# Written order for attention's last pair, a five-step decode of the first expert block, and a halved last output tile

## The chip, the cores and the metric

The kernel runs on one core of one Trainium2 chip. The metric is the device time of one execution in microseconds; lower is better. Engines are named as in the profile: PE (matrix products), DVE (vector), ACT (scalar), POOL (GpSimd) and SP, which here only issues transfers.

## What is computed

Clustered attention (2 batches, 8 heads, 768 positions, head dimension 64), then two dense expert layers on the 1536 tokens:

```python
mask = q_assign[:, :, :, None] == k_assign[:, :, None, :]     # nearest of 16 centroids
scores = np.where(mask, scale * np.matmul(q, k.transpose(0, 1, 3, 2)), -1e9)
attn = softmax(scores);  x = (attn @ v) as [1536, 512]
x = leaky_relu(x @ w_in1, 0.01) @ w_out1                       # 512 -> 2048 -> 512
out = relu(x @ w_in2) ** 2 @ w_out2
```

All inputs are float32. Every product is made from a rounded high part and a rest (names ending in h and l), so each expert product is three matmuls and each attention-times-values product is two.

## The kernel before

**Attention.** Two heads form a pair; there are NP = 8 pairs. A head's 768 queries go in three units of 256, so a pair has UPP = 6 units and there are NU = 48. A step u of the loop at line 712 runs one line of the table PLAN, in which an entry `Name:lag` calls the operation for unit u - lag. The operations of a unit are, with their engine: S0, S1 (PE, L389: scores of 128 queries, tile S, two buffers); R0, R1 (DVE, L412: row maximum nm); X0, X1 (ACT, L422: exponential e); RE (ACT, L433) and RC (DVE, L436: reciprocal r of the row sums); N0, N1 (POOL, L439: normalise e); Ta, Tb, Tc (PE, L452: four transpositions each into tile T, three buffers); Ha, Hb, Hc (ACT, L463: high part eh); La, Lb, Lc (DVE, L469: rest el); Va, Vb, Vc (PE, L487: four matmuls each into tile A, one buffer); FC (ACT, L500) and FA (DVE, L509), which add A's two halves into xt. With the lags, step u computes scores of unit u + 1, transpositions of u - 2 and products A of u - 3; FA is that of u - 4, and the A of u - 3 starts only when that FA has freed the one buffer. The first three units of a pair belong to its first head and their FA uses partitions 0 to 63, the last three belong to the second head and use 64 to 127. In the first seven pairs, steps also prepare the next pair (dots, cluster ranks L318 to L339, splits). When a pair is done, xsplit (L205, L517 on POOL) splits its xt into xh and xl.

**Who sets the order.** Inside `manual_schedule` each engine's queue stands as the calls are written. Outside, a scheduler sets it by its own estimates. SP is in written order throughout. For the other four engines the first manual block ends at line 719, at step 42, that is ahead of the last pair; a second starts at expert step (0, 2). Between them the scheduler decides.

**Expert blocks.** A weight block (128 x 1024 float64) arrives as raw integer words wraw (one buffer, L147) and is decoded by seven pieces (decode_pieces, L138): load (SP), mag (ACT, L156), shift (DVE, L160), low (DVE, L166), sign (DVE, L173), high (ACT, L133, makes wh) and the rest (POOL, L134, makes wl). For block 0, one piece each follows steps 42 to 46 and two follow step 47 (lines 737 to 741). The load of the next block waits for a small POOL copy of the reciprocals of unit 45 into wraw (L205). The first layer's products h (L770) then fill PE between the last units of attention, as the scheduler places them.

**Output.** g2 (L829) makes four output tiles o of 128 x 512 for a token block, each from two blocks f with three matmuls per f (L847). After the second f, flush (L857) adds o to acc on DVE (L874 for the last step of the second layer) and SP sends 256 KB (L876). Twelve such transfers form the result.

Of the kernel before, what the change touches and what calls it, by code (L numbers as in the profile page):

```python
# [53 lines left out]
def attention_moe_moe_kernel(  # L54
# [9 lines left out]
    nc = tc.nc  # L64
# [7 lines left out]
    NF = w1.shape[0]  # L72
    NU = NP * 2 * (KC // 2)
    UPH = KC // 2
    HALF = S // 2
    N = 512
    NBLK = NT // N
    PLAIN = (3, 2)
    EARLY = 1
# [58 lines left out]
    def decode_pieces(ci):  # L138

        m, f, j = blocks[ci]  # L140
        st = {}

        def load():
            st["raw"] = stg[0].tile([128, 2 * DM, 2], I32, tag="wraw", name="wraw")
            if ci == EARLY:
                pool_copy(out=st["raw"][:, 0].bitcast(F32), in_=r_t[NU - 3])
            nc.sync.dma_start(  # L147
                out=st["raw"].rearrange("p a b -> p (a b)"), in_=(w1, w2)[m][f + j].bitcast(I32)
            )

        def mag():
            pool = stg[0] if j == 0 or ci < 2 else stg[1]
            t = pool.tile([128, 2 * DM], I32, tag="wt", name="wt")
            st["t"] = t
            words[ci] = t.bitcast(F32)
            nc.scalar.mul(out=t.bitcast(F32), in_=st["raw"][:, :, 1].bitcast(F32), mul=W_SHIFT)  # L156

        def shift():
            t = st["t"]
            nc.vector.tensor_scalar(  # L160
                out=t, in0=t, scalar1=3, scalar2=None, op0=ALU.logical_shift_left
            )

        def low():
            t = st["t"]
            nc.vector.scalar_tensor_tensor(  # L166
                out=t, in0=st["raw"][:, :, 0], scalar=29, in1=t,
                op0=ALU.logical_shift_right, op1=ALU.bitwise_or,
            )

        def sign():
            t = st["t"]
            nc.vector.scalar_tensor_tensor(  # L173
                out=t, in0=st["raw"][:, :, 1], scalar=-0x80000000, in1=t,
                op0=ALU.bitwise_and, op1=ALU.bitwise_or,
            )

        def high():
            st["rest"] = split_block(ci, st["t"].bitcast(F32))

        return [load, mag, shift, low, sign, high, lambda: st["rest"]()]
# [22 lines left out]
    def pool_copy(out, in_):  # L204
        nc.gpsimd.tensor_scalar(  # L205
            out=out, in0=in_, scalar1=1.0, scalar2=1.0, op0=ALU.mult, op1=ALU.mult
        )
# [313 lines left out]
    UPP = 2 * UPH  # L521
# [186 lines left out]
        "pl11": lambda p: place(p, 1, 1),  # L708
    }

    early = [f for i in range(EARLY) for f in decode_pieces(i)]
    for u in range(-1, NU + 5):
        if u == NU - UPP:
            pst.close()
            stg.append(ctx.enter_context(tc.tile_pool(name="stg", bufs=1, side="right", reuse_waits="tile")))
            wpx = ctx.enter_context(tc.tile_pool(name="wpx", bufs=SIDE, side="right", reuse_waits="tile"))
            ring.append((wpx, SIDE))
        if u == NU - 6:
            manual.close()
        p = u // UPP  # L720
        for op in PLAN[FIRST[u] if p == 0 else u % UPP].split():
            if ":" in op:
                name, lag = op.split(":")
                i = u - int(lag)
                if 0 <= i < NU and (name, i) != ("RC", 0):
                    unit_ops[name](i)
                    for f in hooks.get((name, i), ()):
                        f()
            else:
                name, ahead = op.split("@")  # L730
                q = p + 1 + int(ahead)
                if name in ("xhi", "xlo"):
                    if 0 <= q - 2 < NP - 1:
                        xsplit(q - 2, name == "xlo")
                elif 0 < q < NP and not (q == 1 and name in PRE):
                    prep_ops[name](q)
        w = u - (NU - UPP)
        if w >= 0:
            k = len(early)
            for f in early[k * w // UPP : k * (w + 1) // UPP]:  # L740
                f()
    xsplit(NP - 1, 0)
    xsplit(NP - 1, 1)
    ast.close()
# [10 lines left out]
    acc = accp.tile([128, NBLK, 4, N], F32, name="acc")  # L755
# [3 lines left out]
    def tmp(tag="q", bufs=6):  # L759
        return gp.tile([128, N], F32, tag=tag, name=tag, bufs=bufs)  # L760

    def bank(i):
        return ps_h.tile([128, N], F32, tag=f"h{i}", name="h")
# [63 lines left out]
    outs = {}  # L827

    def g2(m, b, f):  # L829
        first, last = f % 2 == 0, f % 2 == 1  # L830
        wh, wl = weights[m, f // 2 * 2, f % 2]
        gh, gl = parts.pop((m, b, f))
        for o in range(4):
            if first:
                outs[o] = (ps_l if o == 3 else ps_o).tile([128, N], F32, tag=f"o{o}", name="o")
            if m == 0:
                ws = slice(DM + o * 128, DM + (o + 1) * 128)
                mm = ((wh[:, ws], gh), (wh[:, ws], gl), (wl[:, ws], gh))
            else:
                ts = slice(o * 128, (o + 1) * 128)  # L840
                mm = (
                    (gh[:, ts], wh[:, DM:]),
                    (gh[:, ts], wl[:, DM:]),
                    (gl[:, ts], wh[:, DM:]),
                )
            for i, (l, r) in enumerate(mm):
                nc.tensor.matmul(  # L847
                    out=outs[o],
                    lhsT=l,
                    rhs=r,  # L850
                    start=(first and i == 0),
                    stop=(last and i == 2),
                )
            if last:
                flush(m, b, f // 2, o, outs[o])

    def flush(m, b, g, o, ps):  # L857
        a = acc[:, b, o]
        if g == 0:
            nc.scalar.copy(out=a, in_=ps)  # L860
            return
        if g < NF // 2 - 1:
            nc.vector.tensor_tensor(out=a, in0=ps, in1=a, op=ALU.add)  # L863
            return
        if m == 0:
            c = slice(b * N, (b + 1) * N)
            nc.vector.tensor_tensor(out=a, in0=ps, in1=a, op=ALU.add)
            nc.scalar.copy(out=xh[:, o, c], in_=a)
            nc.gpsimd.tensor_tensor(
                out=xl[:, o, c], in0=a, in1=xh[:, o, c].bitcast(F32), op=ALU.subtract  # L870
            )
        else:
            ob = tmp()
            nc.vector.tensor_tensor(out=ob, in0=ps, in1=a, op=ALU.add)  # L874
            r = b * N + o * 128
            nc.sync.dma_start(out=out[r : r + 128, :], in_=ob)  # L876

    def quad(m, f):
        f0, f1, s = ((m, f, j) for j in range(3))
# [232 lines left out]
```

## Time and profile before

| what | value |
| --- | --- |
| three runs | 762.56 us median, 762.07 to 762.88 |
| the profiled execution | 762.55 us, of which the span of its instructions is 760.8 us |
| PE busy | 746.1 us, 98% of the span |
| DVE busy | 569.7 us, 75% |
| ACT busy | 440.4 us, 58% |
| POOL busy | 383.4 us, 50% |
| granted TensorE clock | 1.000 of full speed |

Busy time counts a matmul until its result is written, and consecutive matmuls overlap, so a busy PE may still issue below its pace. The pace is read from the start of one instruction to that of the next. Of the profile's views, the chain of waits tells what released each instruction on the way to the end, the timeline gives start and duration of single instructions (a row may merge equal ones that follow each other), and the table by stretches gives each engine's busy time between two moments.

### The profile page before, as it was taken

The page shows a single profiled execution, that of the slowest core. Times are in us where ns is not written, and L with a number is a line of the kernel's source. Part 1 is how long each engine was busy: PE and PEld are TensorE (multiplying, and loading weights), DVE is VectorE, ACT ScalarE, POOL GpSimd, SP SyncE. Part 2 cuts the span into 40 slices and gives each one's busy share as a digit, 9 for nine tenths or more (in the row PEclk, how much of TensorE's full clock was granted, in tenths as well). Part 3 has the DMA queues.
Part 4 walks back from the last instruction along what each step waited for, and adds up shares of the span by engine and source line. Part 5 has one row for each costly group of instructions (what it writes and reads, how often), then busy time and mean ns, then how long its engine had stood idle before and what let it go on. Part 6 is the DMA issues. An engine that isn't in the chain of part 4 may idle for free.

```text
span 760.8 us, 11079 instructions
## 1 busy us (share of the span) xinstructions
PE 746.1 (98%) x4060; PEld 650.0 (85%) x4060; DVE 569.7 (75%) x861; ACT 440.4 (58%) x812; POOL 383.4 (50%) x344
## 2 busy tenths in 40 slices
PE   8999999999999999999999999999999999999998
PEld 8899999999989888888888888887878888888886
DVE  5999999999999545876666576656678787686755
ACT  6988988988998564344444343546544345443430
POOL 2889889889855326561442314356461441423400
PEclk9999999999999999999999999999999999999999
DMA  7494563572601212111121112203111211122004
GB/s 230 96 219 110 123 167 107 123 170 69 154 23 61 107 56 111 55 56 56 59 108 56 55 56 84 83 1 111 56 56 61 94 68 55 56 77 90 1 1 165
DMA packets 16902, 66.35 MB, mean 87 GB/s; under 512 B 3152, under 2 KB 4048, under 8 KB 11856
## 3 DMA queue, kind: packets, MB, share of 16 engines
q1 hardware_dynamic: 16848, 65.65, 29.1%
q8 instruction: 32, 0.52, 0.3%
q14 instruction: 22, 0.18, 0.1%
HBM read 44.60 MB, written 3.15 MB: 63 GB/s over the span
## 4 chain that ended last, share of the span: by engine, by line
PE 78%; DVE 13%; ACT 5%; issue 1%; DMA 1%; POOL 1%; DVEq 0%; SPq 0%; ACTq 0%; POOLq 0%
PE o L847 32%; PE h L770 29%; PE A L487 6%; PE S L389 5%; PE T L452 5%; DVE el L469 4%; DVE nm L412 3%; ACT e L422 2%; DMA wraw<-w 1%; PE warm L242 1%; DVE xt L509 1%; DVE ds L319 1%; ACT acc L860 1%; DVE m L318 1%; DVE h L806 1%
## 5 line engine op out<-in xcount | busy, mean ns | idle before, releaser
L134 POOL TENSOR_TENSOR wl<-wt,wh 128x1024 fp32r<-128x1024 f32 x32 | 77.0, 2407 | 132.8 <-ACT wh L133 132.8
L818 DVE TENSOR_TENSOR gl<-h,gh 128x512 fp32r<-128x512 f32 x96 | 65.8, 690 | 70.8 <-ACT h L813 50.2
L770 PE MATMUL h<-xl,wh 128*128 128x512 f32 x296 | 115.4, 390 | 0.0
L770 PE MATMUL h<-xh,wl 128*128 128x512 f32 x296 | 115.0, 389 | 0.0
L770 PE MATMUL h<-xh,wh 128*128 128x512 f32 x296 | 114.8, 390 | 0.0
L863 DVE TENSOR_TENSOR acc<-o,acc 128x512 f32<-128x512 f32 x144 | 92.6, 685 | 12.1 <-PE o L847 12.1
L469 DVE TENSOR_TENSOR el<-T,eh 128x512 fp32r<-128x512 f32 x144 | 94.4, 683 | 4.3 <-ACT eh L463 3.2
L439 POOL TENSOR_SCALAR e<-e,r 128x768 f32<-128x768 f32 x96 | 87.7, 925 | 19.4 <-DVE r L436 13.2
L412 DVE TENSOR_REDUCE nm<-S 128x1 f32<-128x768 f32 x96 | 90.9, 948 | 4.2 <-PE S L297 2.4
L422 ACT ACTIVATE e<-S,nm 128x768 f32<-128x768 f32 x96 | 87.3, 909 | 11.0 <-DVE nm L412 6.8
L389 PE MATMUL S<-hb 128*128 128x384 f32 (+1 forms) x384 | 90.2, 349 | 1.9 <-ACT e L422 1.2
L463 ACT CAST eh<-T 128x512 fp32r<-128x512 f32 x144 | 79.8, 589 | 13.4 <-PE T L452 13.1
L487 PE MATMUL A<-eh,vv 128*128 128x256 f32 x288 | 79.6, 306 | 2.0 <-DVE xt L509 2.0
L452 PE MATMUL T<-ident,e 128*128 128x128 f32 x576 | 79.6, 273 | 1.0 <-DVE el L469 1.0
L847 PE MATMUL o<-wh,gh 128*128 128x512 f32 x192 | 75.0, 391 | 2.8 <-DVE acc L863 1.7
L847 PE MATMUL o<-gl,wh 128*128 128x512 f32 x192 | 74.8, 390 | 0.0
L847 PE MATMUL o<-wh,gl 128*128 128x512 f32 x192 | 74.7, 389 | 0.0
L847 PE MATMUL o<-gh,wl 128*128 128x512 f32 x192 | 74.7, 389 | 0.0
L847 PE MATMUL o<-wl,gh 128*128 128x512 f32 x192 | 74.7, 389 | 0.0
L847 PE MATMUL o<-gh,wh 128*128 128x512 f32 x192 | 73.6, 389 | 0.0
L487 PE MATMUL A<-el,vv 128*128 128x256 f32 x288 | 72.5, 282 | 0.4 <-DVE el L469 0.4
L452 PEld LDWEIGHTS T<-ident,e 128*128 128x128 f32 x576 | 69.0, 144 | 4.0 <-POOL e L439 1.3
(130 smaller groups left out, 1537.1 us busy)
## 6 DMA issues: line engine op xcount, KB each, us to landing
wraw<-w SPq DMA_DIRECT2D x32, 1024.0 KB, 4.7
hb<-spl SPq DMA_DIRECT2D x14, 576.0 KB, 4.7
hb<-spl SPq DMA_DIRECT2D x42, 192.0 KB, 5.1
rqk<-qk SPq DMA_DIRECT2D x16, 384.0 KB, 3.8
rv<-v SPq DMA_DIRECT2D x8, 384.0 KB, 3.6
out<-q SPq DMA_DIRECT2D x12, 256.0 KB, 2.0
twice<-qk SPq DMA_DIRECT2D x8, 192.0 KB, 6.3
hb<-st SPq DMA_DIRECT2D x56, 24.0 KB, 2.0
```

The lines of the kernel that those rows point to most:

```text
L134: return lambda: nc.gpsimd.tensor_tensor(out=wl, in0=t, in1=wh.bitcast(F32), op=ALU.subtract)
L389: nc.tensor.matmul(out=s[:, c, 0:HALF], lhsT=hb[0:k, a, i * 128 : (i + 1) * 128], rhs=hb[0:k, b, c * HALF : (c + 1) * HALF], start=(a == 0 ...
L412: nc.vector.tensor_reduce(out=n, in_=s_t[t][:, :, 0:HALF], axis=AX.XY, op=ALU.max, negate=True)
L422: nc.scalar.activation(out=e.rearrange("p (a b) -> p a b", a=2), in_=s_t.pop(t)[:, :, 0:HALF], func=AF.Exp, bias=n_t.pop(t), scale=1.0, ac ...
L439: nc.gpsimd.tensor_scalar(out=e_t[t], in0=e_t[t], scalar1=r_t[t // 2][:, t % 2 : t % 2 + 1], scalar2=1.0, op0=ALU.mult, op1=ALU.mult,)
L452: nc.tensor.transpose(T[:, o : o + 128], e_t[2 * u + b][:, kc * 128 : (kc + 1) * 128], ident)
L463: nc.scalar.copy(out=eh[:, 2 * g : 2 * g + 2, :].rearrange("p a b -> p (a b)"), in_=T_t[u, g])
L469: nc.vector.tensor_tensor(out=el[:, 2 * g : 2 * g + 2, :].rearrange("p a b -> p (a b)"), in0=T_t.pop((u, g)), in1=eh[:, 2 * g : 2 * g + 2, ...
L487: nc.tensor.matmul(out=A, lhsT=w, rhs=m[:, kc, :], start=(kc == 0 and i == 0), stop=(kc == KC - 1 and i == 1),)
L770: nc.tensor.matmul(out=out, lhsT=l, rhs=r, start=(first and i == 0), stop=(i == n - 1), skip_group_check=not first,)
L847: nc.tensor.matmul(out=outs[o], lhsT=l, rhs=r, start=(first and i == 0), stop=(last and i == 2),)
L863: nc.vector.tensor_tensor(out=a, in0=ps, in1=a, op=ALU.add)
```

## The change

Three edits. The first manual block is left at step 47 and not at 42, so that the queues of PE, DVE, ACT and POOL keep the written order for steps 42 to 46. The pieces that decode block 0 are called in the middle of a step, behind Lc: load and mag in step 42, shift in 43, low in 44, sign in 45, high and rest in 46, nothing in 47. And of the last output tile (second layer, last token block, last f pair, o = 3) the 512 columns are made as two halves of 256 in two PSUM banks, each with its own matmuls, addition and transfer of 128 KB.

```diff
--- before.py
+++ after.py
@@ -708,14 +708,15 @@
         "pl11": lambda p: place(p, 1, 1),
     }
 
-    early = [f for i in range(EARLY) for f in decode_pieces(i)]
+    early = decode_pieces(0)
+    early_at = (early[0:2], early[2:3], early[3:4], early[4:5], early[5:7], ())
     for u in range(-1, NU + 5):
         if u == NU - UPP:
             pst.close()
             stg.append(ctx.enter_context(tc.tile_pool(name="stg", bufs=1, side="right", reuse_waits="tile")))
             wpx = ctx.enter_context(tc.tile_pool(name="wpx", bufs=SIDE, side="right", reuse_waits="tile"))
             ring.append((wpx, SIDE))
-        if u == NU - 6:
+        if u == NU - 1:
             manual.close()
         p = u // UPP
         for op in PLAN[FIRST[u] if p == 0 else u % UPP].split():
@@ -726,6 +727,9 @@
                     unit_ops[name](i)
                     for f in hooks.get((name, i), ()):
                         f()
+                if name == "Lc" and NU - UPP <= u < NU:
+                    for f in early_at[u - (NU - UPP)]:
+                        f()
             else:
                 name, ahead = op.split("@")
                 q = p + 1 + int(ahead)
@@ -734,11 +738,6 @@
                         xsplit(q - 2, name == "xlo")
                 elif 0 < q < NP and not (q == 1 and name in PRE):
                     prep_ops[name](q)
-        w = u - (NU - UPP)
-        if w >= 0:
-            k = len(early)
-            for f in early[k * w // UPP : k * (w + 1) // UPP]:
-                f()
     xsplit(NP - 1, 0)
     xsplit(NP - 1, 1)
     ast.close()
@@ -831,6 +830,7 @@
         wh, wl = weights[m, f // 2 * 2, f % 2]
         gh, gl = parts.pop((m, b, f))
         for o in range(4):
+            split = (m, b, f // 2, o) == (1, NBLK - 1, NF // 2 - 1, 3)
             if first:
                 outs[o] = (ps_l if o == 3 else ps_o).tile([128, N], F32, tag=f"o{o}", name="o")
             if m == 0:
@@ -843,19 +843,25 @@
                     (gh[:, ts], wl[:, DM:]),
                     (gl[:, ts], wh[:, DM:]),
                 )
-            for i, (l, r) in enumerate(mm):
-                nc.tensor.matmul(
-                    out=outs[o],
-                    lhsT=l,
-                    rhs=r,
-                    start=(first and i == 0),
-                    stop=(last and i == 2),
-                )
-            if last:
-                flush(m, b, f // 2, o, outs[o])
-
-    def flush(m, b, g, o, ps):
-        a = acc[:, b, o]
+            todo = [(outs[o], slice(0, N))]
+            if split:
+                if first:
+                    outs[4] = bank(0)
+                todo = [(outs[3 + j][:, 0 : N // 2], slice(j * N // 2, (j + 1) * N // 2)) for j in range(2)]
+            for ps, c in todo:
+                for i, (l, r) in enumerate(mm):
+                    nc.tensor.matmul(
+                        out=ps,
+                        lhsT=l,
+                        rhs=r[:, c],
+                        start=(first and i == 0),
+                        stop=(last and i == 2),
+                    )
+                if last:
+                    flush(m, b, f // 2, o, ps, c)
+
+    def flush(m, b, g, o, ps, part):
+        a = acc[:, b, o, part]
         if g == 0:
             nc.scalar.copy(out=a, in_=ps)
             return
@@ -870,10 +876,10 @@
                 out=xl[:, o, c], in0=a, in1=xh[:, o, c].bitcast(F32), op=ALU.subtract
             )
         else:
-            ob = tmp()
+            ob = tmp()[:, part]
             nc.vector.tensor_tensor(out=ob, in0=ps, in1=a, op=ALU.add)
             r = b * N + o * 128
-            nc.sync.dma_start(out=out[r : r + 128, :], in_=ob)
+            nc.sync.dma_start(out=out[r : r + 128, part], in_=ob)
 
     def quad(m, f):
         f0, f1, s = ((m, f, j) for j in range(3))
```

**DVE, steps 42 to 44 of the last pair.** nm is a row maximum, el a rest of a transposed tile, xt is FA, r a reciprocal; wt is the block being decoded. Before:

```order
L160 TENSOR_SCALAR wt_3367<-wt_3367 128x1024
L469 TENSOR_TENSOR el_3260<-T_3270,eh_3259 128x512
L166 SCALAR_TENSOR_TENSOR wt_3367<-wraw_3304,wt_3367 128x1024
L509 TENSOR_TENSOR xt_3098<-A_3253,xt_3098 64x256
L412 TENSOR_REDUCE nm_3325<-S_3293 128x1
L469 TENSOR_TENSOR el_3260<-T_3299,eh_3259 128x512
L436 RECIPROCAL r_3249<-r_3249 128x2
L173 SCALAR_TENSOR_TENSOR wt_3367<-wraw_3304,wt_3367 128x1024
L412 TENSOR_REDUCE nm_3352<-S_3328 128x1
```

The change, from `shift` in step 43 to behind `low` in step 44:

```order
L160 TENSOR_SCALAR wt_3266<-wt_3266 128x1024
L469 TENSOR_TENSOR el_3324<-T_3307,eh_3323 128x512
L412 TENSOR_REDUCE nm_3354<-S_3330 128x1
L469 TENSOR_TENSOR el_3324<-T_3335,eh_3323 128x512
L509 TENSOR_TENSOR xt_3098<-A_3317,xt_3098 64x256
L436 RECIPROCAL r_3313<-r_3313 128x2
L412 TENSOR_REDUCE nm_3388<-S_3358 128x1
L469 TENSOR_TENSOR el_3324<-T_3364,eh_3323 128x512
L166 SCALAR_TENSOR_TENSOR wt_3266<-wraw_3264,wt_3266 128x1024
L469 TENSOR_TENSOR el_3386<-T_3369,eh_3385 128x512
```

The three operations on wt stood within eight rows; now each is alone in its step, behind one el and ahead of another.

**POOL, end of the last pair.** Rows on e normalise two tiles of a unit (e_3436 is the first of unit 45 in both); xh and xl split the seventh pair's xt; wl is the rest of block 0. Before:

```order
L134 TENSOR_TENSOR wl_3608<-wt_3367,wh_3607 128x1024
L439 TENSOR_SCALAR e_3311<-e_3311,r_3312 128x768
L439 TENSOR_SCALAR e_3338<-e_3338,r_3312 128x768
L205 TENSOR_SCALAR xh_66<-xt_3098 128x768
L439 TENSOR_SCALAR e_3374<-e_3374,r_3375 128x768
L439 TENSOR_SCALAR e_3401<-e_3401,r_3375 128x768
L517 TENSOR_TENSOR xl_67<-xt_3098,xh_66 128x768
L439 TENSOR_SCALAR e_3436<-e_3436,r_3437 128x768
L439 TENSOR_SCALAR e_3463<-e_3463,r_3437 128x768
L205 TENSOR_SCALAR wraw_3764<-r_3437 128x2
```

The change:

```order
L439 TENSOR_SCALAR e_3374<-e_3374,r_3375 128x768
L205 TENSOR_SCALAR xh_66<-xt_3098 128x768
L439 TENSOR_SCALAR e_3402<-e_3402,r_3375 128x768
L517 TENSOR_TENSOR xl_67<-xt_3098,xh_66 128x768
L205 TENSOR_SCALAR wraw_3764<-r_3437 128x2
L134 TENSOR_TENSOR wl_3519<-wt_3266,wh_3518 128x1024
L439 TENSOR_SCALAR e_3436<-e_3436,r_3437 128x768
L439 TENSOR_SCALAR e_3464<-e_3464,r_3437 128x768
```

The row on wl stood ahead of unit 43's normalisation; it now stands ahead of unit 45's, behind the split of the seventh pair and the copy into wraw.

**PE, behind the last scores.** S_3546 and S_3550 are unit 47's second score tile; T tiles that read e_3436 are unit 45's transpositions; A_3572 is unit 44's product. Before:

```order
L452 MATMUL T_3558<-ident_70,e_3436 128x128
L452 MATMUL T_3558<-ident_70,e_3463 128x128
L452 MATMUL T_3558<-ident_70,e_3436 128x128
L452 MATMUL T_3558<-ident_70,e_3463 128x128
L389 MATMUL S_3546<-hb_3002 128x384 x4
L452 MATMUL T_3580<-ident_70,e_3436 128x128
L452 MATMUL T_3580<-ident_70,e_3463 128x128
```

The change:

```order
L452 MATMUL T_3556<-ident_70,e_3402 128x128
L452 MATMUL T_3562<-ident_70,e_3436 128x128
L452 MATMUL T_3584<-ident_70,e_3436 128x128
L487 MATMUL A_3572<-eh_3512,vv_3079 128x256
L487 MATMUL A_3572<-el_3513,vv_3079 128x256
```

Unit 45's first transpositions stood ahead of the last scores, where now they stand behind them; they are still ahead of unit 44's product.

## Rows read from the trace of the kernel before

**Rows 1.** The page, part 4: the chain that ended last, by engine.

```profile
PE 78%; DVE 13%; ACT 5%; issue 1%; DMA 1%; POOL 1%; DVEq 0%; SPq 0%; ACTq 0%; POOLq 0%
```

**Rows 2.** Busy time by stretch: us, PE, PEld, DVE, ACT, POOL, clock, DMA, GB/s.

```profile
205.16:209.33 4.17, 4.17 (x34) 4.10 (x33) 4.17 (x8) 4.02 (x11) 4.12 (x4) 1.00 0.57 175
...
262.00:510.00 248.00, 248.00 (x1095) 205.07 (x1094) 158.90 (x206) 114.87 (x180) 98.35 (x67) 1.00 0.18 64
```

**Rows 3.** The chain in order of time (start, us, what): pieces on PE.

```profile
206.49 0.95 PE A L487 x8
...
207.44 0.71 PE S L389 x4
...
208.15 0.88 PE T L452 x8
...
286.78 2.72 PE o L847 x12
```

**Rows 4.** Busy time of PE from unit 38 to the second output block.

```profile
208.78:267.34 58.56, 57.23 (x372) 1.00 0.19 69
```

**Rows 5.** Timeline of PE (start, us, engine, line, op, tiles, idle before): its two idle spells.

```profile
220.25 0.38 PE L487 MATMUL A<-el,vv 128*128 128x256 f32 x1 [0.35 <-DVE el L469]
...
223.00 1.23 PE L452 MATMUL T<-ident,e 128*128 128x128 f32 x8 [0.98 <-DVE el L469]
```

**Rows 6.** Timeline of DVE: R1 of steps 38, 39, 40 and 42, a pair of rests.

```profile
196.20 0.96 DVE L412 TENSOR_REDUCE nm<-S 128x1 f32<-128x768 f32 x1
...
200.51 0.96 DVE L412 TENSOR_REDUCE nm<-S 128x1 f32<-128x768 f32 x1
...
204.47 0.93 DVE L412 TENSOR_REDUCE nm<-S 128x1 f32<-128x768 f32 x1
...
212.44 0.94 DVE L412 TENSOR_REDUCE nm<-S 128x1 f32<-128x768 f32 x1
...
213.54 0.69 DVE L469 TENSOR_TENSOR el<-T,eh 128x512 fp32r<-128x512 f32 x1 [0.16 <-ACT eh L463]
```

**Rows 7.** The chain in order of time: pieces on DVE, and a product behind one.

```profile
195.05 0.46 DVE m L330
...
195.55 0.44 DVE xt L509
...
196.03 0.74 PE A L487 x4
...
215.61 0.68 DVE wt L160
...
216.90 1.13 DVE wt L166
...
220.27 1.12 DVE wt L173
```

**Rows 8.** Timeline of ACT, steps 42 and 43: mag, a high part, an exponential.

```profile
213.88 1.16 ACT L156 ACTIVATE wt<-wraw 128x1024 f32<-128x1024 f32 x1
...
214.91 0.60 ACT L463 CAST eh<-T 128x512 fp32r<-128x512 f32 x1
...
216.82 0.90 ACT L422 ACTIVATE e<-S,nm 128x768 f32<-128x768 f32 x1
```

**Rows 9.** Timeline of POOL in the last pair, and one DVE row beside it.

```profile
212.37 1.79 POOL L439 TENSOR_SCALAR e<-e,r 128x768 f32<-128x768 f32 x2 [1.89 <-PE S L389]
...
220.44 2.61 POOL L439 TENSOR_SCALAR e<-e,r 128x768 f32<-128x768 f32 x2 [6.28 <-DVE r L436]
...
223.02 2.38 POOL L134 TENSOR_TENSOR wl<-wt,wh 128x1024 fp32r<-128x1024 f32 x1
...
241.09 1.17 DVE L160 TENSOR_SCALAR wt<-wt 128x1024 int32<-128x1024 int32 x1 [0.45 <-ACT wt L156]
```

**Rows 10.** Timeline of the end, and transfers: issuer, count, KB each, us to landing.

```profile
755.69 2.37 SPq L876 DMA_DIRECT2D out<-q  x4
...
out<-q SPq DMA_DIRECT2D x12, 256.0 KB, 2.0
```

## The prediction

> **What bounds the kernel now.** I read the page's chain first: 78% of it is PE and 13% DVE [rows 1], so the order of work on PE decides, and DVE only where PE waits for it. The table by stretches then says where PE has room. From 262 to 510 us it is busy for all of 248.00 us [rows 2], at full clock; behind the place of the change nothing can be caught up, so a delay (or gain) at attention's end moves the end of the kernel by the same amount. What has to be weighed is the stretch from the last pair to the first expert products.
>
> There PE's own pace comes from starts on the chain: eight products A take 0.95 us (0.119 each), four scores 0.71 (0.178), eight transpositions 0.88 (0.110), twelve expert products 2.72 (0.227) [rows 3]. A unit of 12 A, 12 T and 8 S is 4.17 us of PE, and the stretch of that length in the written order shows PE busy throughout [rows 2]. From the first A of unit 38 to the first o of the second output block 58.56 us go by [rows 4]. In them lie 120 A, 105 T, 48 S and 96 h or o: 14.25 + 11.55 + 8.52 + 21.76 = 56.08 us. So the scheduler's order loses **2.5 us** there; 1.3 of it is visible as two waits of PE for DVE's rests el [rows 5], the rest is smaller than a view shows. This is all that a better order could win here.
>
> The rival resource is DVE. From one step's first row maximum to the next it takes 200.51 to 204.47, 3.96 us, and 196.20 to 200.51, 4.31, where FA belongs to a pair's second head [rows 6]. Against 4.17 DVE has only 0.2 us to spare in the former and is over in the latter. Before, the scheduler placed the decoding among shifted work; in the written order it comes on top of a full step.
>
> **The inserts on DVE.** Steps 43, 44 and 45 carry FA of units 39 to 41 (second head), 46 that of unit 42 (first head). The three inserted operations take some 0.60 (the next starts 0.60 after the shift's start; its row says 0.68), 1.13 and 1.12 us [rows 7]. In step 42 nothing is added on DVE, but mag stands on ACT between Ha and X1. It starts at 213.88 and holds ACT until 214.91, 1.03 us [rows 8]. Behind it X1 (0.90) and Hb (0.60) end at 214.91 + 1.50 = 216.41, and DVE, free for that el at 215.61 [rows 7], waits 0.80. A further 0.16 is the wait for ACT of the first el of this step [rows 6], which I keep. From R1 of step 42 at 212.44 [rows 6], which the change does not touch, R1 comes at
> - step 43: 212.44 + 4.31 + 0.16 + 0.80 = 217.71
> - step 44: + 4.31 + 0.60 = 222.62
> - step 45: + 4.31 + 1.12 = 228.05
> - step 46: + 3.96 + 1.12 = 233.13
>
> FA stands just ahead of R1, and A has one buffer. That PE feels a late FA at once is seen in an ordinary pair: a mask operation of 0.46 us on DVE, FA at 195.55, and A at 196.03 directly behind it [rows 7]. So unit 43's first A comes at about 233.1. At PE's pace it would come five units after unit 38's, at 208.78 + 5 x 4.17 = 229.63 [rows 2, 4]. **Lost: 3.5 us.** X1 behind mag also delays a score tile by some 0.25; that lies within these 3.5.
>
> **Step 46.** `high` is a pass over 128 x 1024 on ACT like mag, so about 1.03 us [rows 8]; it stands ahead of X1, which frees the S buffer for unit 47's second scores. By the pace these would start at 233.1 + 0.48 + 0.71 + 0.44 + 0.95 = 235.7; they come about 0.2 later. Then `rest` runs on POOL, from about 235.2 for 2.38 us [rows 9], to 237.6; behind it in POOL's queue is unit 45's normalisation, the first of a pair that takes 1.79 [rows 9], so about 0.9, to 238.5. In PE's order unit 45's transpositions come directly behind the last scores and ahead of unit 44's products. The scores end near 236.0 + 0.71 + 0.44 = 237.1, so PE waits **1.4 us**, and nothing stands in its queue that could go first. Together with the 0.2: 1.6. Then h products cover what DVE still has to do. The other moved work (xl of the seventh pair, the copy into wraw, the second block's load) runs in front of that point or under 21 h products (21 x 0.227 = 4.8 us); I cost it at nothing, and price the case in which that cover is too short as a rival.
>
> **DVE beside POOL.** No row shows an inserted operation at its new place. By the steps above each starts some 0.3 us before POOL ends a normalisation pair. A shift at 241.09 beside one took 1.17 instead of 0.68; a normalisation pair beside `sign` took 2.61 instead of 1.79 [rows 7, 9]. One of two therefore waits. The bounds are 0 (POOL gives way each time) and 3 x 0.3 = 0.9; I take **0.6**, since the shift's row is the nearest and shows DVE giving way, by more than 0.3. The Trainium skill, "SBUF — State Buffer", section "SBUF: two separate sides", says that a DVE operation with two SBUF inputs (or in a two-port mode) and a GpSimd operation share a pair of ports by an exclusive lock: the one that starts first keeps it for its whole instruction, and the other stands still. By that rule each of the three inserts waits out its 0.3, the term is 0.9 and the time would be 766.0; the trace agrees so far that 2.61 is 1.79 + 0.82.
>
> **The halved tile.** Three products of 512 columns, 3 x 0.227 = 0.68 us, become six of 256, each like an A product: 6 x 0.119 = 0.71, so +0.03 for a pass and +0.07 for its two passes [rows 3]. The last addition begins as late as before but is half as long. SP hands on the last transfers about 0.6 us apart (four in 2.37 [rows 10]), mostly at the pace of the additions, and one transfer more costs it up to that. A transfer of 256 KB lands 2.0 us after its issue [rows 10]; no row shows one of 128 KB at the end. Bounds: -0.4 (half an addition and a little of the landing saved) to +0.4 (a further issue, nothing saved). I take **-0.1**.
>
> **Sum.** 3.5 + 1.6 + 0.6 - 2.5 - 0.1 = +3.1 us. The profiled execution took 762.55 us, as good as the median of 762.56, so the forecast is **765.7 us**. A change of 0.2%, 1.5 us, is about what this measurement can tell from none: 761.0 to 764.1 counts as the same.
>
> **Rivals.**
> - *Faster: the buffers absorb the inserts.* S has two buffers and T three. If PE can run ahead on transpositions and scores while FA is late, DVE's debt of each insert is paid in parts, only some 0.5 us of the 2.5 stay lost, and the time is 762.55 - 2.0 = **760.5**. It decides whether FA's lateness reaches A, that is whether an insert plus a DVE step exceeds 4.17; even the smallest, 3.96 + 0.60, does, and the A at 196.03 waited at once [rows 7]. For it speaks that the written order ran PE without a gap in every step before [rows 2]. 8%.
> - *No change.* The three waits that no row shows at their new place do not occur: mag's 0.8, the port's 0.6, the 1.4 for `rest`. Then +3.1 - 2.8 = +0.3, **762.9**. For it speaks that each depends on a few tenths of timing on another engine; against it, that all three would have to go. 18%.
> - *Worse: the second block is late.* Its load waits for the copy of unit 45's reciprocals, which now stands behind the split of the seventh pair on POOL, and its decoding must then pass DVE and POOL. If the 21 h products end first, PE waits about a `rest` of 2.38 less what is left of them, some 2 us: **767.7**. Against it: the copy stands ahead of `rest`, and 4.8 us is more than one pass of any engine. 6%.
>
> **How the numbers follow.** My case has 68%, with a range of its own of 764.2 to 767.0: the ends of the unknown terms are 0.6 either way for the ports, 0.5 for the tail and 0.8 for mag. The range reaches over most of the no-change case: **762.4 to 767.2**; outside lie the faster case, most of the worse one and thin edges. Slower: all of my case, the worse one, and a little of the no-change case, 75%. Same: most of the no-change case, 17%. Faster: 8%.
>
> **What the profile after should show.** If I am right, R1 to R1 on DVE in steps 42 to 45 reads about 5.3, 4.9, 5.4 and 5.1, with PE's A idle behind FA (L509) in steps 44 to 46; unit 43's first A at about 233.1; a wait of PE of some 1.4 at a transposition behind a normalisation, near 237 to 238.5; the first o of the second output block near 270.5 instead of 267.3, and everything behind it moved by the same 3.2. If A's starts keep 4.17 through steps 43 to 46, the inserts were absorbed and the first term is wrong; if PE has no wait behind the normalisation, the second; if the offset at 270 is not that of the end, the claim that PE is full behind it fails.

## The result and the profile after

| | before | the change |
| --- | --- | --- |
| median of six runs | 762.44 us | 766.86 us |
| range | 761.85 to 763.07 | 766.01 to 769.33 |
| ratio | | 1.0063, 95% interval 1.0053 to 1.0073 |

The change is slower: by 4.4 us from the medians, by 4.8 from the ratio (0.0063 x 762.4). The forecast was +3.1, 765.7 us, with a range up to 767.2; by the ratio the time (1.0063 x 762.56 = 767.4) lies just beyond it. Direction, place and most of the mechanism were right, the sum was too small.

One thing in the profiled execution of the change (769.33 us) does not belong to the change: the other five took 766.01 to 767.03, with a median of 766.71. Between 10 and 20 us, long before attention's last pair, TensorE was granted 0.69 of full speed, where before it had all of it. The table by stretches shows it, first of the kernel before and then of the change (us, then PE, PEld, DVE, ACT, POOL busy, clock, DMA, GB/s):

```profile
10.00:20.00 10.00, 8.41 (x67) 7.80 (x65) 8.71 (x11) 8.31 (x16) 2.60 (x3) 1.00 0.71 212
```

```profile
10.00:20.00 10.00, 9.67 (x55) 9.17 (x55) 6.51 (x9) 6.58 (x10) 3.16 (x3) 0.69 0.74 215
```

The first A of unit 38 starts at 210.75, where before it started at 208.78, 1.97 us later, and everything behind it with it. So I read all times from that A on. Timeline of PE after, this A and each place where PE loses time (start, us, engine, line, op, tiles, idle before and what ended it):

```profile
210.75 0.36 PE L487 MATMUL A<-eh,vv 128*128 128x256 f32 x1
...
217.98 0.97 PE L389 MATMUL S<-hb 128*128 128x384 f32 x4 [0.23 <-ACT e L422]
...
224.88 0.39 PE L487 MATMUL A<-eh,vv 128*128 128x256 f32 x1 [0.82 <-DVE xt L509]
...
230.66 0.39 PE L487 MATMUL A<-eh,vv 128*128 128x256 f32 x1 [1.20 <-DVE xt L509]
...
236.22 0.39 PE L487 MATMUL A<-eh,vv 128*128 128x256 f32 x1 [1.07 <-DVE xt L509]
...
239.18 0.98 PE L389 MATMUL S<-hb 128*128 128x384 f32 x4
240.00 0.60 PE L452 MATMUL T<-ident,e 128*128 128x128 f32 x4
241.64 0.44 PE L452 MATMUL T<-ident,e 128*128 128x128 f32 x2 [1.04 <-POOL e L439]
241.83 0.36 PE L487 MATMUL A<-eh,vv 128*128 128x256 f32 x1
...
273.76 1.20 PE L853 MATMUL o<-gh,wh 128*128 128x512 f32 x4 [0.31 <-ACT gh L811]
```

The chain that ended last has moved a little from PE to DVE and ACT [rows 1]; from the page, part 4, and its part 6 for the last transfers (issuer, count, KB each, us to landing):

```profile
PE 75%; DVE 14%; ACT 6%; DMA 2%; issue 1%; POOL 1%; SPq 0%; DVEq 0%; ACTq 0%; POOLq 0%
```

```profile
out<-q SPq DMA_DIRECT2D x2, 128.0 KB, 1.9
```

The half transfers land after 1.9 us, the whole ones after 2.0 [rows 10]. On PE, three products A wait for DVE's FA, one transposition for POOL's normalisation. The two waits of before for el [rows 5] are gone, as forecast, and there is a new one at the first o of the second output block. From unit 38's A to that o it is 273.76 - 210.75 = 63.01 us instead of 58.56 [rows 4]: **+4.45** of the loss stands in this stretch. I call its length "the stretch" below; it doesn't depend on the start of the run.

Timeline of DVE after: R1 of steps 42 to 46 and the three inserts, each with the row behind it:

```profile
214.43 0.93 DVE L412 TENSOR_REDUCE nm<-S 128x1 f32<-128x768 f32 x1
...
219.81 0.96 DVE L412 TENSOR_REDUCE nm<-S 128x1 f32<-128x768 f32 x1
...
221.28 1.03 DVE L160 TENSOR_SCALAR wt<-wt 128x1024 int32<-128x1024 int32 x1
222.23 0.67 DVE L469 TENSOR_TENSOR el<-T,eh 128x512 fp32r<-128x512 f32 x1
...
225.05 0.96 DVE L412 TENSOR_REDUCE nm<-S 128x1 f32<-128x768 f32 x1
...
226.53 1.55 DVE L166 SCALAR_TENSOR_TENSOR wt<-wraw,wt 128x1024 int32<-128x1024 int32 x1
228.00 0.68 DVE L469 TENSOR_TENSOR el<-T,eh 128x512 fp32r<-128x512 f32 x1
...
230.83 0.96 DVE L412 TENSOR_REDUCE nm<-S 128x1 f32<-128x768 f32 x1
...
232.30 1.47 DVE L173 SCALAR_TENSOR_TENSOR wt<-wraw,wt 128x1024 int32<-128x1024 int32 x1
233.70 0.68 DVE L469 TENSOR_TENSOR el<-T,eh 128x512 fp32r<-128x512 f32 x1
...
236.16 0.92 DVE L412 TENSOR_REDUCE nm<-S 128x1 f32<-128x768 f32 x1
```

R1 to R1 is 5.38, 5.24, 5.78 and 5.33; I had worked out 5.27, 4.91, 5.43 and 5.08, with the wait beside POOL as a term of its own. The inserts take 0.95, 1.47 and 1.40 to the start of the next row, against 0.60, 1.13 and 1.12 before [rows 7]: **0.97 us longer together**. What POOL does at those moments (timeline of POOL after):

```profile
219.97 1.79 POOL L439 TENSOR_SCALAR e<-e,r 128x768 f32<-128x768 f32 x2 [3.48 <-PE T L452]
225.21 1.80 POOL L439 TENSOR_SCALAR e<-e,r 128x768 f32<-128x768 f32 x2 [3.45 <-DVE r L436]
230.99 0.91 POOL L439 TENSOR_SCALAR e<-e,r 128x768 f32<-128x768 f32 x1 [3.98 <-DVE r L436]
231.87 0.83 POOL L205 TENSOR_SCALAR xh<-xt 128x768 fp32r<-128x768 f32 x1
232.68 1.87 POOL L439 TENSOR_SCALAR e<-e,r 128x768 f32<-128x768 f32 x1
...
238.32 2.38 POOL L134 TENSOR_TENSOR wl<-wt,wh 128x1024 fp32r<-128x1024 f32 x1 [1.74 <-ACT wh L133]
240.69 3.98 POOL L439 TENSOR_SCALAR e<-e,r 128x768 f32<-128x768 f32 x4
```

The first pair ends at 221.76, 0.48 after shift's start, the second at 227.01, 0.48 after low's, xh at 232.70, 0.40 after sign's; low ends 1.07 and sign 1.07 behind POOL's end, where alone they take about 1.22. So each insert loses its overlap with POOL's operation, less 0.12 to 0.14 us. The normalisation behind xh then takes 1.87 instead of 0.91: it ends 0.78 behind sign. At the end rest (238.32) holds unit 45's normalisation until 240.69, and PE's transposition starts at 241.64.

### The profile page after: what moved, and what is told of

Same layout as the page of the kernel before. It is cut to its first block, busy times and chain, and to the rows that moved or that the text cites. A ratio compares the mean times of both kernels' runs of the same rounds, so it can differ in the third digit from the quotient of the medians.

```text
span 767.5 us, 11089 instructions
## 1 busy us (share of the span) xinstructions
PE 750.5 (98%) x4066; PEld 653.2 (85%) x4066; DVE 572.3 (75%) x862; ACT 440.5 (57%) x812; POOL 384.7 (50%) x344
## 4 chain that ended last, share of the span: by engine, by line
PE 75%; DVE 14%; ACT 6%; DMA 2%; issue 1%; POOL 1%; SPq 0%; DVEq 0%; ACTq 0%; POOLq 0%
PE o L853 30%; PE h L769 28%; PE A L487 5%; PE S L389 5%; PE T L452 4%; DVE el L469 4%; DVE nm L412 3%; ACT e L422 2%; DMA wraw<-w 1%; DVE wt L166 1%; DVE xt L509 1%; ACT wt L156 1%; ACT eh L463 1%; ACT acc L866 1%; DVE wt L173 1%
```

## The experiments

All are edits of the changed kernel unless it says otherwise. The table gives the ratio to the kernel before, run on the same chip, and the stretch, worked out from the starts in each profile's timeline of PE.

| kernel | median, us | before, us | ratio (95%) | stretch, us |
| --- | --- | --- | --- | --- |
| before | | | | 58.56 |
| the change | 766.86 | 762.44 | 1.0063 (1.0053 to 1.0073) | 63.01 |
| no_dve_decode | 763.23 | 761.87 | 1.0017 (1.0006 to 1.0028) | 59.20 |
| dve_behind_la | 766.41 | 761.87 | 1.0055 (1.0038 to 1.0072) | 62.60 |
| rest_behind_norm | 765.27 | 761.87 | 1.0041 (1.0026 to 1.0056) | 61.65 |
| high_rest_late | 764.55 | 761.87 | 1.0036 (1.0025 to 1.0047) | 61.50 |
| mag_behind_hb | 766.25 | 762.28 | 1.0054 (1.0036 to 1.0072) | 62.87 |
| fold_on_act_pool | 765.12 | 762.28 | 1.0041 (1.0027 to 1.0054) | 61.24 |
| tail_alone | 762.32 | 762.28 | 1.0003 (0.9994 to 1.0012) | 58.54 |
| place_alone | 762.54 | 762.02 | 1.0007 (0.9998 to 1.0017) | 58.54 |
| order_alone | 764.49 | 762.28 | 1.0035 (1.0021 to 1.0050) | 60.50 |
| order_to_44 | 764.13 | 762.02 | 1.0026 (1.0015 to 1.0037) | 59.88 |
| order_alone_xl_late | 763.02 | 762.02 | 1.0017 (1.0007 to 1.0026) | 59.83 |
| order_mag_on_pool | 762.89 | 762.43 | 1.0004 (0.9995 to 1.0013) | 59.07 |

In the diffs of early_at a key now names the operation behind which, and the step in which, the pieces of that number (0 load, 1 mag, 2 shift, 3 low, 4 sign, 5 high, 6 rest) are called. They are written short here: the code has NU - UPP + 0 for 42 and so on, and the loop that calls the pieces is left out.

**Is it DVE's load?** no_dve_decode never calls the three DVE pieces of block 0:

```diff
-    early_at = (early[0:2], early[2:3], early[3:4], early[4:5], early[5:7], ())
+    early_at = {("Lc", 42): (0, 1), ("Lc", 46): (5, 6)}
```

> The three DVE operations that decode block 0 are left out (its values are then wrong); all else as in the change. Theory (DVE has no room in a full step, so an insert and its wait beside POOL reach A in full): R1 to R1 on DVE in steps 43 to 45 falls from 5.24, 5.78 and 5.33 to about 4.3, 4.3 and 4.0, PE's 3.1 us of waiting for FA (L509) shrink to under 0.6, and some 3.8 us come back: 763.1 us, 762.3 to 763.8. Rival (the written order with A's one buffer loses the time in any case): the waits for FA stay above 2 us and the time above 765.5.

The waits of PE from 205 to 300 us (engine, line, for what: us in total, times, longest):

```profile
PE T L452 <- POOL e L439: 1.0, 1, 1.0
PE S L389 <- ACT e L422: 0.4, 2, 0.2
PE o L852 <- ACT gh L810: 0.3, 1, 0.3
```

The waits for FA are gone altogether and the stretch is 63.01 - 59.20 = 3.81 us shorter, the number expected and the length of the three inserts (0.95 + 1.47 + 1.40 = 3.82). So the inserts and their waits are paid for in full, and the written order without them doesn't make PE wait for FA at all.

**Do they wait for POOL?** dve_behind_la moves shift, low and sign behind La:

```diff
+    early_at = {("Lc", 42): (0, 1), ("La", 43): (2,), ("La", 44): (3,), ("La", 45): (4,), ("Lc", 46): (5, 6)}
```

> The change, with shift, low and sign called behind La (one rest later in DVE's queue), when POOL has ended the pair of normalisations. Theory (the inserts are long because they wait for POOL's operation to end): shift and low fall from 1.03 and 1.55 us to about 0.68 and 1.2; sign meets a later normalisation, which xh pushes back in that step, and keeps its length or grows; 766.2 us, 765.7 to 766.6. Rival (they are long for another reason, such as the transfers or their operands): the three durations stay and so does the time, 766.9.

Timeline of DVE there:

```profile
220.12 0.68 DVE L160 TENSOR_SCALAR wt<-wt 128x1024 int32<-128x1024 int32 x1
...
225.02 1.22 DVE L166 SCALAR_TENSOR_TENSOR wt<-wraw,wt 128x1024 int32<-128x1024 int32 x1
...
230.46 1.76 DVE L173 SCALAR_TENSOR_TENSOR wt<-wraw,wt 128x1024 int32<-128x1024 int32 x1
```

Shift and low are as short as expected, sign is longer, since in its step xh pushes the second normalisation back onto it. The stretch is 0.41 shorter; the total is not to be told from the change.

**What does rest's place cost?**

```diff
+    early_at = {("Lc", 42): (0, 1), ("Lc", 43): (2,), ("Lc", 44): (3,), ("Lc", 45): (4,), ("Lc", 46): (5,), ("N1", 46): (6,)}
```

> The change, with rest (POOL, wl of block 0) called behind unit 45's normalisation and not ahead of it. Theory of the prediction (rest holds unit 45's normalisation, and that holds PE 1.0 to 1.4 us): the wait goes, 765.7 us. Rival, which I now hold likelier: FA of unit 43, behind R1 of step 47 on DVE, comes at the same moment (in the change it ends 0.25 us before the waiting A starts), so the wait only changes its name from POOL's e to DVE's xt, and no more than 0.3 us is won: 766.6.

The waits of PE:

```profile
PE A L487 <- DVE xt L509: 3.2, 4, 1.2
PE S L389 <- ACT e L422: 0.2, 1, 0.2
```

Both theories were half right. The wait for POOL does change its name to FA, and unit 44's A starts only 0.25 us earlier (30.83 instead of 31.08 behind unit 38's). But in that time PE has now made transpositions that in the change came after it, so the work is not lost: the stretch is 1.36 shorter, of which 0.46 is the wait at the second output block, gone too. The mistake of the second theory was to price a wait by the start of one instruction, and not by what PE had done by then.

high_rest_late also calls high behind Hb:

```diff
+    early_at = {("Lc", 42): (0, 1), ("Lc", 43): (2,), ("Lc", 44): (3,), ("Lc", 45): (4,), ("Hb", 46): (5,), ("N1", 46): (6,)}
```

> As the run before (rest behind unit 45's normalisation), and high (ACT, wh of block 0) behind Hb of step 46 instead of ahead of X1. If high ahead of X1 delays unit 47's last scores and through them R1, FA and A: PE's wait for X1 (0.3 us) and DVE's wait for Hb (0.5 us) go, A of unit 44 starts about 0.7 us earlier than in the run before, 765.9 us, 765.4 to 766.3. If ACT has room there: as the run before.

Unit 44's A starts at 30.41 (-0.42), of which 0.15 is left in the stretch: less than the 0.7 expected. The time, 764.55 against 765.27, points the same way within the intervals.

**mag.**

```diff
+    early_at = {("Lc", 42): (0,), ("Hb", 42): (1,), ("Lc", 43): (2,), ("Lc", 44): (3,), ("Lc", 45): (4,), ("Lc", 46): (5, 6)}
```

> The change with mag (ACT) called behind Hb of step 42 and not ahead of X1. Theory (mag ahead of X1 and Hb makes DVE wait 0.77 us for Hb and PE 0.4 for S): both waits go, the exponential of step 43 comes up to 1.0 us later, half of the gain is kept: R1 to R1 of step 42 falls from 5.38 to about 4.6, 766.2 us. Rival (ACT has no room in a full step, so the 1.03 us only move to the next one): 766.9, with a wait for X0 of step 43 in its place.

Timeline of DVE there, R1 of step 42, the FA of step 43 and its R1:

```profile
211.40 0.93 DVE L412 TENSOR_REDUCE nm<-S 128x1 f32<-128x768 f32 x1
...
216.04 0.43 DVE L509 TENSOR_TENSOR xt<-A,xt 64x256 f32<-64x256 f32 x1 [0.81 <-ACT xt L500]
...
216.70 0.96 DVE L412 TENSOR_REDUCE nm<-S 128x1 f32<-128x768 f32 x1
```

R1 to R1 is 5.30 and not 4.6: the wait of 0.8 only moves from el to FA, which follows ACT's FC. The rival holds, on two runs and this row: ACT has no room for 1.03 us in that step at either place.

**Less DVE work instead of fewer inserts.** fold_on_act_pool stands on high_rest_late and takes four FA off DVE:

```diff
+    FOLDS = dict.fromkeys(range(39, 43))
...
+        if u in FOLDS:
+            y = FOLDS[u] = sm.tile([128, 256], F32, tag="fa", name="fa", bufs=2)[64 * j : 64 * j + 64]
+            nc.scalar.copy(out=y, in_=a_t.pop(u)[64 * j : 64 * j + 64])
...
+        if u in FOLDS:
+            y = FOLDS[u]
+            hooks[("N0" if u == NU - 7 else "N1", u + 3)] = [lambda: nc.gpsimd.tensor_tensor(out=x, in0=y, in1=x, op=ALU.add)]
+            return
```

> On top of high_rest_late: A's second half of units 39 to 42 is copied out by ACT behind FC (64 x 256, 0.37 us) and added on POOL, so that DVE loses four FA (0.43 us each, and the 0.2 to 0.3 around those of a second head) in the very steps that carry the inserts. Theory (DVE's load in those steps sets A's pace): R1 to R1 falls to about 4.5, 5.0 and 4.6 in steps 43 to 45, PE's waits for FA from 3.1 to about 1.3 us, 762.9 us, 762.2 to 763.6. Rival (ACT, with 0.15 us of room in a step, becomes the bound): no more than 0.5 us won, 764.0, and PE waits for X.

The two longest waits of PE, and a row of its timeline of ACT:

```profile
PE S L389 <- ACT e L422: 1.2, 3, 0.7
PE T L452 <- POOL e L439: 0.6, 1, 0.6
```

```profile
226.33 0.90 ACT L422 ACTIVATE e<-S,nm 128x768 f32<-128x768 f32 x1 [0.83 <-DVE nm L412]
```

No wait for FA is left, but at a ratio of 1.0041 it isn't better than high_rest_late's 1.0036: PE now waits for ACT's exponentials. R1 to R1 is 5.46, 5.20 and 5.14 in steps 43 to 45, and not 4.5, 5.0 and 4.6. In step 43 DVE waits 0.84 us for ACT's eh, as the rival has it. Behind that ACT itself stands idle for DVE's row maximum (0.83 in the row above), and DVE has no such wait from 219.56 to 231.96. So the wait has in part only changed its name: ACT is the bound in the step behind mag, and DVE with its inserts (1.44 for low and 1.46 for sign, beside POOL again) in the two that follow.

**The halved tile.** tail_alone is the kernel before with this part alone.

> The kernel before with the halved last output tile alone. My term: -0.1 us (0.07 more on PE, some 0.15 less behind the last product): the same as before within 0.3 us. Rival (a further issue on SP and a short transfer that is no quicker): +0.3 to +0.6.

1.0003 (0.9994 to 1.0012): nothing, within the 0.3 us expected. My -0.1 can't be told from zero.

**Order and place apart.** place_alone leaves the manual block at step 42 as before, and keeps the new places; order_alone keeps the written order to step 47 and calls the pieces where the kernel before does.

The edit of place_alone:

```diff
-        if u == NU - 1:
+        if u == NU - 6:
```

That of order_alone, in place of the calls behind Lc:

```diff
+        w = u - (NU - UPP)
+        if w >= 0:
+            k = len(early)
+            for f in early[k * w // UPP : k * (w + 1) // UPP]:
+                f()
```

> The change without the longer written order: the manual block is left at step 42 as before, the pieces are called at the change's places (and the halved tile is kept). It completes a square: before 762.4, order alone +2.2, both +4.4. Theory (the two parts do different harm: the order keeps PE from going round a late FA, the places put inserts beside POOL's normalisation and rest ahead of unit 45's): the scheduler, free to place the rows by itself, does most of what it did before, 763.0, 762.3 to 764.0, and PE's waits for FA stay under 1 us. Rival (the places cost their 2.2 us in any order): 764.6 or more.

> The change with the decoding where the kernel before calls it: one piece at the end of each of steps 42 to 46 and two after step 47, in the written order (the halved tile kept). Theory (the debt is DVE's, whatever step it falls in): the inserts still cost PE their length, but behind Lb they miss POOL's normalisations, so PE's waits for FA are some 0.6 us smaller than in the change; block 0 is ready a step later, so the first h comes later and PE has less to fill with: 766.0 to 768.5, not under 765. Rival (the time is lost because the pieces were moved, not because the order is kept): about 762.5.

place_alone is the kernel before again: its stretch is 58.54, and its waits of PE are the old ones:

```profile
PE T L452 <- DVE el L469: 1.0, 1, 1.0
PE A L487 <- DVE el L469: 0.3, 1, 0.3
```

Where the calls stand means nothing here as long as the scheduler sets the order. order_alone costs 0.35%, less than expected, and I was wrong about it: the h products come earlier than in the change (31.59 behind unit 38's A instead of 33.61). Of these 2.02 us, 1.27 are won by unit 43's first A (24.20 instead of 25.47), which sign, a step later, no longer delays, and 0.50 more by unit 44's, where rest no longer stands ahead of unit 45's normalisation. Of the 0.63% the order alone brings 0.35; the places, harmless by themselves, bring the rest once the order holds them.

In order_alone, low met the rest xl of the seventh pair. Its DVE and POOL rows:

```profile
230.14 2.11 DVE L166 SCALAR_TENSOR_TENSOR wt<-wraw,wt 128x1024 int32<-128x1024 int32 x1
```

```profile
229.34 1.83 POOL L517 TENSOR_TENSOR xl<-xt,xh 128x768 fp32r<-128x768 f32 x1
```

xl ends at 231.17; low ends at 232.25, 1.08 later. order_alone_xl_late moves xl behind the next normalisation:

```diff
-                    if 0 <= q - 2 < NP - 1:
+                    if u == NU - 2:
+                        hooks[("N1", u - 1)] = [lambda: xsplit(NP - 2, 1)]
+                    elif 0 <= q - 2 < NP - 1:
```

> order_alone with the rest xl of the seventh pair (POOL, two inputs) called behind the normalisation of step 46 instead of ahead of it, so that low on DVE no longer meets it. If an inserted operation stands still until POOL's operation ends (low took 2.11 us there, starting 1.03 us before xl ended): low falls to about 1.2, PE's wait of 1.8 us for FA to about 0.9, sign then meets xl for some 0.3 us; 763.9 us, 763.4 to 764.3. If low is long there for another reason: 764.5.

Timeline of DVE there:

```profile
229.66 1.22 DVE L166 SCALAR_TENSOR_TENSOR wt<-wraw,wt 128x1024 int32<-128x1024 int32 x1
```

low takes 1.22, PE's longest wait for FA 0.9 instead of 1.8, and the kernel 763.02 us: 0.9 us better than expected by the time, and by the stretch (-0.67) as expected.

**How many written steps?** order_to_44 is order_alone with the manual block left at step 44.

> order_alone with the manual block left at step 44 instead of 47. Theory (each written step that carries an insert costs about what the insert takes, since PE's next product stands behind a late FA): with only steps 42 and 43 written, and no insert on DVE in them, most of the 2.2 us of order_alone go: 762.8 us, 762.0 to 763.6, so about the kernel before. Rival (the first written steps, with mag on ACT, carry the loss): 764 or more.

764.13, against the 762.8 expected: leaving earlier gains little. The scheduler puts all three inserts between two R1, 221.31 and 228.94 in the timeline of DVE, and PE waits 1.2 us for el and 0.4 for gh. Neither theory says this; how much of it is chance of the scheduler's order stays open.

**The best written order.** order_mag_on_pool adds to order_alone_xl_late that POOL makes mag of block 0:

```diff
+            raw = st["raw"][:, :, 1].bitcast(F32)
+            if ci < EARLY:
+                nc.gpsimd.tensor_scalar(
+                    out=t.bitcast(F32), in0=raw, scalar1=W_SHIFT, scalar2=1.0, op0=ALU.mult, op1=ALU.mult
+                )
+                return
...
```

> order_alone_xl_late with mag of block 0 on POOL (a multiplication behind the normalisation of step 43, where POOL is idle for some 2.5 us) instead of ACT. Theory (mag's 1.07 us on ACT delays the next exponential, and with it the scores and R1 of that step): PE's wait of 0.5 us for ACT goes, and with it some 0.3 of the later waits for FA; 762.2 us, 761.7 to 762.8, no longer to be told from the kernel before (762.0 to 762.5). Rival (POOL's multiplication takes over 2.3 us, so that shift waits for it, or the wait only moves to the next exponential): 763.0 or more.

Its POOL row, and all that PE waits for from 205 to 300 us:

```profile
218.29 1.12 POOL L158 TENSOR_SCALAR wt<-wraw 128x1024 f32<-128x1024 f32 x1
```

```profile
PE A L493 <- DVE xt L515: 1.7, 3, 0.9
```

POOL needs 1.12 us for it, and PE's wait for ACT is gone. At 1.0004 (0.9995 to 1.0013) this written order can't be told from the kernel before by its time: of the change's 0.63% all but noise is taken back by moving xl, high, rest and mag and keeping the pieces at the ends of their steps. Its stretch is still 0.51 us longer. It does not beat the kernel before: no version here does. What stays are the waits for FA, 1.7 us.

## Why the prediction was right and wrong

The forecast failed in three terms: the inserts' wait beside POOL was put too low, a wait at the second output block was costed at nothing, and what the written order gives back was put too high.

**Right: the mechanism of the inserts.** DVE is full in a written step, an insert reaches A through FA, and PE behind it is full, so nothing is caught up. no_dve_decode gives the inserts' 3.8 us back to the tenth. The rival that the buffers absorb the inserts is out: the three waits for FA stand in the rows of the profile after. PE's loss up to unit 43's first A is 236.22 - 210.75 - 5 x 4.17 = 4.62 us; I had 3.5 + 0.6 = 4.1.

**Mis-sized: "DVE beside POOL".** I took 0.6 within bounds of 0 and 0.9; the rows show 0.97. The halfway value came from "one of two waits": I let POOL give way part of the time. The rows say who does: the one that starts later, DVE's inserts in three cases of three. The Trainium skill, "SBUF — State Buffer", section "SBUF: two separate sides", states this lock, and by it the term was 0.9; here the trace agrees with who waits, in the change (0.35 + 0.34 + 0.28), in low beside xl (2.11, and 1.22 when xl was moved) and for POOL too (1.87 instead of 0.91 behind sign). That 0.9 comes so near to 0.97 is in part luck: the overlaps were 0.48, 0.48 and 0.40 and not 0.3 each, and each cost 0.12 to 0.14 less than its length. The lock's sum of 766.0 was still below the measurement: at the inserts it accounts for 0.4 of what was missing.

**Right in size: step 46.** I had 1.6 for high and rest. The scores start at 239.18 where the last A's end was due at 238.89 (0.29 late), and the transposition at 241.64 where four of 0.11 behind 240.00 end at 240.44 (1.20 late): 1.49. rest_behind_norm took back 1.36 of stretch, of which 0.46 is the wait at the second output block, and not by the route that either theory gave.

**Wrong: "Then h products cover what DVE still has to do", costed at nothing.** At the second output block PE waits for ACT's gh. The product before it starts at 273.07, so the o was due 0.227 later, at 273.30; it comes at 273.76, some 0.46 late. The chain that ended last passes through this place, by way of the fourth weight block's decoding (start, us, what):

```profile
267.64 2.76 DVE wt L166
...
270.42 1.24 DVE wt L173
...
271.68 1.05 ACT wh L133
...
273.22 0.51 ACT gh L811
```

That low takes 2.75 us in the timeline, and not 1.22, since it starts beside the xl that splits the last pair (timeline of POOL):

```profile
267.14 2.16 POOL L517 TENSOR_TENSOR xl<-xt,xh 128x768 fp32r<-128x768 f32 x1
```

xl ends at 269.30 and low 1.09 later. So this wait is the inserts' wait over again, at a place that I had not looked at: the 1.5 us that low loses there are more than the 0.46 that PE waits. The same pair of rows (2.75 and 2.16 or 2.17) and the same wait stand in no_dve_decode, dve_behind_la and mag_behind_hb, which like the change have rest just ahead of unit 45's normalisation; in the ten other profiles that low takes 1.22 or 1.23. Of those ten only order_to_44 has a wait for gh too, and there the chain goes back to the load of that block. No run moves that xl by itself, and by what steps rest's place brings the two together was not followed. My rival on a late second block named this kind of wait and put it at 6% and 2 us; it came in part, in the likeliest case and not as a case of its own.

**Mis-sized: "So the scheduler's order loses 2.5 us there", all of it given back.** In the stretch, the change loses 4.62 + 1.49 + 0.46 = 6.57 and is 4.45 longer, so 2.12 came back. The 2.5 was a difference of two large sums (58.56 and 56.08), made with rates for each kind of matmul; a part was in no order to be won. The two idle times of [rows 5] alone, 0.35 and 0.98, would have given a lower bound of 1.3, and I took the other end.

Together: +0.5 at the inserts (of which 0.4 beside POOL), -0.1 in step 46, +0.5 at gh and +0.4 less given back turn the 3.2 forecast for the stretch into 4.45. By the last product another 0.4 is lost: 0.2 at the rests gl right behind that gh (the first product with gl comes 1.22 behind the first o, where before it was 1.01), and 0.07 by the halved tile's extra PE time; the rest I did not trace.

The **range** was too narrow above for one reason: each of these terms had a bound on the same side (DVE waits, cover is short, less comes back), and I let the range lean toward the no-change rival instead, whose three waits all occurred. It is refuted by the rows of after, wait by wait.

## What to carry to other kernels

Before work is put into a fixed order, compare the step's length on each engine, not its share of the span: an engine with 0.2 us to spare in a 4.17 us step pays an insert in full. Moving work to the next engine helps only where that one has room in the same step: ACT had none for mag, POOL had. In a fixed order look at which operation of another engine is under way when the insert starts, and do it for the later blocks too: here the same decoding cost 0.63% at one set of places in the steps, 0.17% at another, and with mag on POOL nothing that the time can show. And where a scheduler sets the order, moving a call tests nothing; look at the instruction order before pricing it.

## What the runs showed of the hardware

A decoding operation on DVE and an operation on POOL did not share time here: the later one waited for the earlier to end, and lost what was left of it, less 0.12 to 0.14 us. Rows: low 2.11 us beside xl, of which 1.03 were left, and 1.22 without; low of the fourth block 2.75 where 1.66 of an xl were left; sign 1.76 beside a normalisation in dve_behind_la, of which 0.68 were left, and 1.21 alone in order_alone; a normalisation 1.87 behind sign, of which 1.09 were left, instead of 0.91. I had expected POOL to give way some of the time.

The granted clock of TensorE was 0.69 between 10 and 20 us in the one profiled run of the change: 0.50 from 10 to 16 us, the lower of its two levels (1.2 and 2.4 GHz), and 1.00 from 7 to 9 and again from 17 us on. Ahead of it PE had waited for a transfer (timeline of PE):

```profile
7.09 3.29 PE L297 MATMUL dots<-cbd,rqk 128*128 128x32 f32 x24 [0.28 <-DMA rqk<-qk]
```

The run of before has no wait there, and the clock was full between 10 and 20 us in every other profile. But fold_on_act_pool has a wait of 0.19 us for the same transfer at full clock, so whether that wait brought it about stays open. So does the exact price: unit 38's first A comes 1.97 us later than before, but in the other twelve profiles it comes anywhere from 207.68 to 209.00.
